# Queries and keys of the last tokens of tiles 8 to 15: computed ahead of the first segment and in segments 1 to 3, instead of in tiles 7 to 14

## The chip, the cores and the metric

The kernel runs on one NeuronCore of a Trainium2 chip. The metric is the device time of one launch, in microseconds. The kernel before takes 1615.39 us, the median of three runs (1613.97 to 1617.68).

## What is computed

Two layers, each made of a part A and a part B, on x of 2048 tokens x 512 features in bf16. Part A is attention with a recurrent memory: the sequence is cut into 64 segments of 32 tokens, and segment s attends over 8 memory rows and its own 32 tokens; the first 8 output rows are the memory of segment s + 1. So the 64 segments are a chain, and only the memory rows are carried along it.

```python
for s in range(n_seg):    # 64, one after the other
    h = jnp.concatenate([mem, xs], axis=1)    # 8 + 32 rows x 512
    q, k, v = (einsum('btd,dhe->bhte', h, W) for W in (Wq, Wk, Wv))   # 32 heads x 128
    scores = where(mask, einsum('bhqe,bhke->bhqk', q, k) * scale, -1e9)
    o = einsum('bhte,hed->btd', einsum('bhqk,bhke->bhqe', softmax(scores), v), Wo)
    mem = o[:, :8, :]; outs.append(o[:, 8:, :])
```

Part B is a gated MLP over the whole sequence (w_in, a 2048 x 2048 mix over the tokens, w_out). Each part is applied to the layer norm of x, and its result is added to x.

## The kernel before

**Tiles, segments, groups.** `a_block` (once per layer) walks the 64 segments. Four segments are a tile of 128 tokens (`tb`, 0 to 15; `j4` is the segment in its tile), four tiles are a group G. The matmuls of a segment itself (`psQ`, `psm`, `psK`, `psV` at L723) use 32 rows: 8 memory rows and the first 24 tokens. The last 8 tokens of a segment do not depend on the memory that is being made, so they are not done there: their queries, keys and values are made a tile at a time, 4 x 8 = 32 rows `hB`, one tile ahead, and put into `QTB`, `KTB` and `VB`/`VX` of that tile. That work comes in six pieces j = 0 to 5 (two halves of Q, of K and of V), 16 matmuls each of 32 weight columns by 512, four of them side by side in the array (`b_mms`, tile `psb`).

**The fill.** The pieces are the fill of the segment loop: `segment` calls `fill()` at three places (ahead of `pv(0)`; behind `spare1`; behind `last_out(0)`), and each call takes one step of a generator `more`. The order of the work on PE, DVE and ACT is the order in which the program states it (`manual_schedule` with ORDERED); SP's and POOL's order is the scheduler's.
- Segment 0 of layer one takes the values (`values`), segments 1 to 3 have `iter(())`: no fill.
- Tiles 1 to 3 (`tb < 4`) use `b_even`: in each segment half a piece in two steps (4 + 4 matmuls) and then a whole piece (16): 24 matmuls per segment. The last piece, j = 1, is turned by a DVE transpose (`turns`, L769), not by a DMA.
- Tiles 4 to 14 use `b_units` in the segments j4 = 0 to 2 (4, 8 and 20 matmuls) and `y_part` in j4 = 3, also 4 + 8 + 20: the product with Wo of the last tokens of the group before (`wo_last`, tile `pwB`), whose sum is added by DVE (`adds`, L857 and L863).
- Both layers use the same two patterns.

**Spare work.** `spare1`, `spare2` and `spare3` hold DVE and ACT work that isn't the segment's: layer norm of rows two tiles ahead (`x_stats`, `rows.apply`), and from tile 8 on the finished rows of eight tiles before (`ys`: in one segment two halves of an addition, `y_half` L238, in the next the statistics `y_stats` L147 and then `y_norm` L249).

**The start of layer one.** All weights come over GpSimd's DMA queue: Wq and Wk in halves r = 0, 1, then Wv (`a_open_qkv_weights`), then Wo in seven transfers (`_Wo.open`); a transfer is issued when the one eight places before it on that queue has landed. Meanwhile PE makes the pieces j = 0, 2 of tiles 0 and 1 and j = 1, 3 of tile 0, each as its half of the weights lands (`b_units(0, 6)`, `units`, and `b_units(1, 2, alone=True)`, `units1`), then segment 0, with the rest of tile 1's pieces in it (`ahead_of_wo`).

**The start of layer two.** At the end of part B, `wo.open(nc.sync)` queues 1.9 MB of Wo on SP's queue and then `ahead.spread` the four transfers that put the values of tile 0 into `VX`.

Of the kernel before, what the change touches and what calls it, by code (L numbers as in the profile page):

```python
# [14 lines left out]
P = 128  # L15
DM = 512
KT = 4
# [25 lines left out]
def _ln_consts(ctx, tc, c):  # L43
    nc = tc.nc
    cp = ctx.enter_context(tc.tile_pool(name="consts_ln", bufs=1))
    eps_t = cp.tile([P, 1], F32, name="eps_t")
    nc.vector.memset(eps_t[:], LN_EPS)
    c["eps_t"] = eps_t
    c["ident_bf"] = _identity(nc, cp)

    c["MV"] = [cp.tile([P, 16, 2], F32, name=f"MV{i}") for i in range(2)]
    c["RS"] = [cp.tile([P, 16], F32, name=f"RS{i}") for i in range(2)]


# [8 lines left out]

def _consts(ctx, tc, c, b_sp):
    nc = tc.nc
# [12 lines left out]
    nc.vector.tensor_reduce(out=is_own[:], in_=fourth[:], op=ALU.max, axis=mybir.AxisListType.X)  # L78
    nc.vector.tensor_copy(own, is_own[:].to_broadcast([P, 4, 16]))
    for q in range(0, P, 32):  # L80
# [104 lines left out]
class _Rows:  # L185


    def __init__(self, nc, pool, xd, xb_d, o_d, x_in):
        self.nc, self.pool, self.xd, self.xb_d, self.o_d, self.x_in = nc, pool, xd, xb_d, o_d, x_in
        self.xs, self.hT, self.y = {}, {}, {}  # L190

# [61 lines left out]
def b_block(tc, c, rows, front, xd, MV_out, RS_out, w_sp, w_out, S, first, ahead, wo, out_final=None):  # L253
# [4 lines left out]
    with ExitStack() as ctx:  # L258
# [231 lines left out]
def kernel(  # L490
# [31 lines left out]
    rows = _Rows(nc, rp, xd, xb_d, o_d, x_in)  # L522
    rows.vb_d = dram.tile([P, 8 * DH], BF16, name="vb_d")
    with tc.manual_schedule(engines=ORDERED):
        _act_table(nc)
        for tt in range(2):
            x = rp.tile([P, DM], F32, name="x0", tag=("ln_x", "y_x")[tt])[:, 0:DM // 2].bitcast(BF16)
            nc.sync.dma_start(x, x_in[tt * P:(tt + 1) * P, :])
            rows.xs[tt] = x
        m0 = rp.tile([2 * M, DM], BF16, name="m0", tag="y_o")  # L530
        nc.vector.memset(m0[:], 0.0)
        nc.sync.dma_start(m0[0:M, :], A_mem0.rearrange("b m d -> (b m) d"))
        rows.m0T = rp.tile([P, KT, 2 * M], BF16, name="m0T")
        wqkv, rest = a_open_qkv_weights(tc, ctx, A_Wq, A_Wk, A_Wv)
        c = {}
        _ln_consts(ctx, tc, c)
        MV, RS = c["MV"], c["RS"]
        with tc.tile_pool(name="turn_ps", bufs=3, space=PSUM) as turn_ps:

            def turn(out, x, n):  # L540
                ps = turn_ps.tile([P, KT * n], BF16, name=f"turn{n}", tag="turn")
                for kt in range(KT):
                    nc.tensor.transpose(ps[:, n * kt:n * kt + n], x[:, P * kt:P * kt + P], c["ident_bf"][0:n, 0:n])
                nc.scalar.copy(out, ps[:].rearrange("p (kt t) -> p kt t", kt=KT))
# [6 lines left out]
        _consts(ctx, tc, c, B_b_sp)  # L551
        rest()
# [16 lines left out]

def a_open_qkv_weights(tc, stack, Wq, Wk, Wv):  # L570
    nc = tc.nc
    wp = stack.enter_context(tc.tile_pool(name="a_wqkv", bufs=1, side="right"))
    w = [wp.tile([P, KT, HD], BF16, name=n) for n in ("Wq_sb", "Wk_sb", "Wv_sb")]

    def load(parts):
        for k, r in parts:
            srcv = (Wq, Wk, Wv)[k].rearrange("(kt p) h e -> p kt (h e)", p=P)
            for kt in range(KT):
                nc.gpsimd.dma_start(w[k][:, kt, 2048 * r:2048 * r + 2048], srcv[:, kt, 2048 * r:2048 * r + 2048])

    load(((0, 0), (1, 0)))
    return w, lambda: load(((0, 1), (1, 1), (2, 0), (2, 1)))

# [10 lines left out]
class _Wo:  # L594
# [4 lines left out]

    def open(self, eng, first=False):  # L600

# [5 lines left out]
        for k in reversed(range(len(WO_LOW))):  # L607
            n = WO_LOW[k]
            t = ctx.enter_context(self.tc.tile_pool(name=f"a_wo{k}", bufs=1, side="right")).tile([P, n, DM], BF16, name=f"Wo{k}")
            for h in range(n):  # L610
                self.parts[ends[k] - n + h] = t[:, h, :]
            self.parts[f"t{k}"] = t
        for k in range(len(WO_LOW)):
            eng.dma_start(self.parts[f"t{k}"][:], self.wov[:, ends[k] - WO_LOW[k]:ends[k], :])
# [63 lines left out]
def a_block(tc, c, rows, front, MV_in, RS_in, MV_out, RS_out, ahead, wo, S, first):  # L678
# [6 lines left out]
    with ExitStack() as ctx:  # L685
# [4 lines left out]
        for i in range(2):  # L690
            at, v = 0, list(front.old()) if i == 0 else []
            for k, n in enumerate(OLD_SIZES if i == 1 else ()):
                v.append(VBr[0] if k == 1 else old.tile([P, n], BF16, name=f"old{at}")[:])
                at += n
            oBr[i] = v[0].rearrange("p (h t) -> p h t", h=H)
            VBr[i] = v[1] if i else v[1].rearrange("p (i r e) -> p i r e", i=4, r=2)
# [39 lines left out]
        KXr = [[pers.tile([P, 4, 32], BF16, name=f"KX{i}{r}") for r in range(2)] for i in range(NKQ)]  # L736
        uT = [pers.tile([P, H, 32], BF16, name=f"uT{i}") for i in range(2)]
        for t in uT:
            (nc.vector if first else nc.gpsimd).memset(t[:], 0.0)
# [59 lines left out]
        def b_even(tb):  # L799

            bs = blk_state[tb]
            for j, others in ((4, (5, 0)), (3, (2, 1))):
                psA = accA.tile([P, 512], F32, name="psb")[:]
                for kt, other in zip((0, 2), others):
# [9 lines left out]
                    yield  # L814

        def wo_pairs(px, lhs):

# [25 lines left out]

        def y_part(G, q, last=False):

# [5 lines left out]
            pwB = accA.tile([P, DM], F32, name="pwB")  # L851
            for k, _ in enumerate(wo_last(parts, pwB)):
                if k in (0, 2):
                    yield

# [20 lines left out]

            adds.append(out)
            yield
# [25 lines left out]
        def prep_segment(s, eng=nc.gpsimd):  # L904
# [11 lines left out]
            seg_state[s] = dict(QQ=QQ, KX=KX, VX=bs["VX"])  # L916

        def fold(px, cross, t1, beside):
# [18 lines left out]
        def segment(s, fill, spare1, spare2, spare3, tail, loads):  # L937
# [177 lines left out]
            wo_pairs(px, uT_cur)  # L1115
            pw = psO[1][:, 0, 384:512]
            if begin:
                wo_rest(pw, uT_cur, hi=wo.low + 8)
                ahead_of_wo()
                wo_rest(pw, uT_cur, lo=wo.low + 8)  # L1120
            else:
                wo_rest(pw, uT_cur)
            cross = wk.tile([P, P], F32, name="cross", bufs=1)
            beside = nc.scalar.copy(cross[0:64, :], px[64:128, 128:256])
            Rt = segp.tile([P, 2, 512], F32, name="Rt", tag="Rt", bufs=1)
# [26 lines left out]
        if first:  # L1152
            for tb in range(2):
                ln_turn(tb, nc.scalar.copy)
            units, units1 = b_units(0, 6), b_units(1, 2, alone=True)
            for gen, n in ((units, 4), (units1, 2), (units, 4)):
                for _ in range(n):
# [27 lines left out]
        for s in range(NSEG):  # L1185
            tb, j4 = s // 4, s % 4
            if first and s == 0:
                more = values(units)
            elif j4 > 0 and tb == NB - 1:
                more = y_part(tb // 4, j4 - 1, last=True)  # L1190
            elif j4 == (3 if tb < NB - 1 else 0) and tb > 3:
# [33 lines left out]
            def spare2():  # L1225
                if first and s == 8:
                    c["cast_bsp"] = c["load_bsp"]()
                if first and s == 12:
                    c["cast_bsp"]()
                for y, added in ys:  # L1230
                    if added:
# [3 lines left out]

            def spare3():
                for y, added in ys:
                    if added:
# [10 lines left out]
            def tail():  # L1249
                if j4 == (3 if first and tb == 0 else 2 if tb < 4 else 1) and tb + 1 < NB:  # L1250
                    ahead.spread(blk_state[tb + 1]["VX"])
# [11 lines left out]

            def loads():
                if due and s < NSEG - 1 and (not ys or tb == NB - 1):
                    y = due.pop(0)
# [69 lines left out]
```

## Time and profile before

| what | value |
|---|---|
| three runs, median (lowest to highest) | 1615.39 us (1613.97 to 1617.68) |
| the profiled execution: its time, its span | 1618.87 us, 1617.1 us |
| between the span and that time | 1.8 us |
| granted TensorE clock, mean | 0.999 |
| busy: PE, PEld, DVE, ACT, POOL | 98%, 61%, 66%, 65%, 19% |
| layer one, segment 0 begins / segment 63 begins | 28.53 us / 672.57 us |
| layer two, segment 0 begins / segment 63 begins | 828.47 us / 1465.15 us |

A segment begins where its first `psQ` matmul does. Times inside the profile are microseconds from the span's start. Matmuls that run side by side are each counted with their own length, so the mean of one is longer than its share of the busy time. In the rows of engines, the first number is the start or the stretch, then the length, and `xN` is the number of instructions.

### The profile page before, as it was taken

The page shows a single profiled execution, that of the slowest core. Times are in us where ns is not written, and L with a number is a line of the kernel's source. Part 1 is how long each engine was busy: PE and PEld are TensorE (multiplying, and loading weights), DVE is VectorE, ACT ScalarE, POOL GpSimd, SP SyncE. Part 2 cuts the span into 40 slices and gives each one's busy share as a digit, 9 for nine tenths or more (in the row PEclk, how much of TensorE's full clock was granted, in tenths as well). Part 3 has the DMA queues.
Part 4 walks back from the last instruction along what each step waited for, and adds up shares of the span by engine and source line. Part 5 has one row for each costly group of instructions (what it writes and reads, how often), then busy time and mean ns, then how long its engine had stood idle before and what let it go on. Part 6 is the DMA issues. An engine that isn't in the chain of part 4 may idle for free.

```text
span 1617.1 us, 91209 instructions
## 1 busy us (share of the span) xinstructions
PE 1579.8 (98%) x41182; PEld 986.2 (61%) x41182; DVE 1066.0 (66%) x3050; ACT 1048.5 (65%) x2281; POOL 301.4 (19%) x667
## 2 busy tenths in 40 slices
PE   5899999999999999999999999999999999999999
PEld 2566666666666666666656666666666666665565
DVE  4577766667776776784456666666677667767722
ACT  3677777777777777660047777777777777776400
POOL 6111111112211221320021111111122122224000
PEclk9999999999999999999999999999999999999999
DMA  9312212213311332377951112212233223425696
GB/s 363 96 43 41 41 43 43 44 43 85 82 47 43 90 89 70 94 182 158 209 174 43 47 43 52 46 48 47 70 93 71 47 75 89 97 52 173 146 197 159
DMA packets 260525, 148.63 MB, mean 92 GB/s; under 512 B 193832, under 2 KB 236432, under 8 KB 260136
## 3 DMA queue, kind: packets, MB, share of 16 engines
q1 hardware_dynamic: 246904, 98.99, 27.5%
q0 software_dynamic: 13232, 43.82, 8.3%
q8 instruction: 322, 5.28, 1.4%
q14 instruction: 67, 0.55, 0.1%
HBM read 59.94 MB, written 37.45 MB: 60 GB/s over the span
## 4 chain that ended last, share of the span: by engine, by line
PE 92%; DMA 4%; issue 1%; DVE 1%; POOL 1%; ACT 0%; SPq 0%; POOLq 0%; DVEq 0%
PE psQ L723 13%; PE psK L723 13%; PE psb L723 10%; PE pg L397 9%; PE psO L828 7%; PE px L821 7%; PE psm L723 6%; PE psV L723 6%; PE pz L296 4%; PE pwB L840 3%; PE psO L1029 3%; PE py L440 2%; PE psT L1021 2%; PE psS L980 2%; DMA Wk_sb<-in_A_Wk_dram 1%
## 5 line engine op out<-in xcount | busy, mean ns | idle before, releaser
L723 PEld LDWEIGHTS <-hT 128*32 128x32 bf16 x12288 | 345.7, 97 | 261.6 <-DVE hT L929 13.9
L723 PE MATMUL psV<-Wv_sb,hT 128*32 128x512 bf16 x2048 | 165.8, 379 | 0.0
L957 DVE STREAM_TRANSPOSE QQ<-rows 128x256 f32<-128x256 f32 x256 | 113.1, 442 | 76.3 <-ACT rows L954 73.8
L954 ACT CAST rows<-psQ 128x512 bf16<-128x512 f32 x256 | 144.2, 591 | 28.9 <-PE psQ L723 26.2
L1050 DVE TENSOR_TENSOR uT<-psO,Rm 128x128 bf16<-128x128 f32 x256 | 74.7, 292 | 126.0 <-ACT Rm L1047 124.1
L989 ACT ACTIVATE S<-psS 128x224 bf16<-128x224 f32 x256 | 92.2, 360 | 96.3 <-PE psS L984 96.1
L397 PE MATMUL pg<-z,wspT 128*128 128x344 bf16 x1024 | 154.3, 309 | 0.0
L957 DVE STREAM_TRANSPOSE KA<-rows 128x256 f32<-128x256 f32 x256 | 113.5, 443 | 61.5 <-ACT rows L954 58.3
L1053 DVE TENSOR_TENSOR uT<-psO,Rt 128x384 bf16<-128x384 f32 x256 | 140.2, 548 | 17.9 <-ACT Rt L1129 15.8
L723 PE MATMUL psK<-Wv_sb,hT 128*32 128x512 bf16 x2048 | 152.0, 378 | 0.0
L1129 ACT ACTIVATE Rt<-Rt 128x512 f32<-128x512 f32 x256 | 147.3, 622 | 4.1
L828 PE MATMUL psO<-Wo_high,uT 128*32 128x128 bf16 x8192 | 141.6, 219 | 3.2 <-issue 3.0
L723 PE MATMUL psQ<-Wq_sb,hT 128*32 128x512 bf16 x2048 | 136.1, 381 | 4.4 <-DVE hT L929 2.8
L723 PE MATMUL psQ<-Wk_sb,hT 128*32 128x512 bf16 x2048 | 135.9, 381 | 0.0
L723 PE MATMUL psm<-Wq_sb,hT 128*32 128x512 bf16 x2048 | 135.1, 379 | 0.0
L723 PE MATMUL psK<-Wk_sb,hT 128*32 128x512 bf16 x2048 | 135.0, 379 | 0.0
L821 PE MATMUL px<-Wo,uT 128*32 128x256 bf16 x3840 | 133.2, 273 | 0.4
L1126 ACT ACTIVATE Rt<-psT 128x1024 f32<-128x1024 f32 x128 | 131.0, 1024 | 3.1
L828 PEld LDWEIGHTS <-uT 128*32 128x32 bf16 x8192 | 125.9, 97 | 11.3 <-issue 6.1
L397 PEld LDWEIGHTS <-wspT 128*128 128x128 bf16 x1024 | 100.0, 98 | 53.5 <-issue 0.4
L821 PEld LDWEIGHTS <-uT 128*32 128x32 bf16 x4096 | 107.6, 97 | 27.5 <-issue 1.3
L914 POOL COPY KX<-old 128x128 bf16<-128x128 bf16 x128 | 66.1, 544 | 274.4 <-PE psS L984 183.6
(202 smaller groups left out, 2875.6 us busy)
## 6 DMA issues: line engine op xcount, KB each, us to landing
o_d<-o_sb SPq DMA_DIRECT2D x126, 64.0 KB
vb_d<-front SPq DMA_DIRECT2D x31, 256.0 KB
VX<-vb_d SPq DMA_DIRECT2D x124, 64.0 KB
ln_x<-xd SPq DMA_DIRECT2D x26, 256.0 KB
y_o<-o_d POOLq DMA_DIRECT2D x22, 256.0 KB, 3.4
xd<-y_o POOLq DMA_DIRECT2D x22, 256.0 KB, 3.0
Wq_sb<-in_A_Wq_dram POOLq DMA_DIRECT2D x8, 512.0 KB, 8.6
Wk_sb<-in_A_Wk_dram POOLq DMA_DIRECT2D x8, 512.0 KB, 10.0
```

What stands on the lines that cost most here:

```text
L397: nc.tensor.matmul(pg[t][:, k, 0:344], lhsT=wsp[t][:, st, :], rhs=z(st, 344 * k, 344 * k + 344), start=(st == 0), stop=(st == NT - 1))
L723: return [nc.tensor.matmul(ps[32 * cg:32 * cg + 32, :], lhsT=lhs(kt, cg), rhs=rhs(kt, cg), start=(kt == 0), stop=(kt == KT - 1), tile_posi ...
L821: nc.tensor.matmul(px[at:at + 32, 0:256], lhsT=lhs[:, h, :], rhs=wo_rhs(h, slice(k + 2, None, -2) if h % 2 else slice(k, None, 2)), start= ...
L828: nc.tensor.matmul(pw[32 * cg:32 * cg + 32, :], lhsT=lhs[:, h, :], rhs=wo_rhs(h, cg), start=False, stop=(h == H - 1), tile_position=(0, 32 ...
L914: eng.tensor_copy(KX[r][:].rearrange("p g (k i) -> p i g k", i=4), bs["KTB"][:, r].rearrange("p (i g) k -> p i g k", i=4)[:, :, :, 8 * j4: ...
L954: return r, mms, copy(r[:].rearrange("p (n el two) -> p n el two", n=8, two=2), ps.rearrange("p (n two el) -> p n el two", n=8, two=2))
L957: nc.vector.transpose(out=(QQ[:, j % 2, :, 0:32] if j < 2 else KA[:, j % 2]).bitcast(F32).rearrange("p n q one -> p n (q one)"), in_=r[:]. ...
L989: return nc.scalar.activation(out=S[:, r], in_=psS[:, r, 0:224], func=ACT.Exp, scale=scale)
L1050: nc.vector.tensor_tensor(out=hview(uT_cur[:], r, 24, 32), in0=oview(r, 0, 8), in1=Rm[:, r].rearrange("p g (n q) -> p g n q", q=8), op=ALU ...
L1053: nc.vector.tensor_tensor(out=hview(uT_nxt[:], r, 0, 24), in0=oview(r, 8, 32), in1=rview(r, 0, 24), op=ALU.mult)
L1126: nc.scalar.activation(out=Rt[:], in_=psT[:], func=ACT.Ln)
L1129: nc.scalar.activation(out=rt, in_=rt, func=ACT.Exp, scale=-1.0)
```

## The change

Only layer one's part A changes in its work, and only for tiles 8 to 15 (groups 2 and 3), pieces j = 0 and j = 2 (first half of Q, first half of K).
- **Gather.** Two DMAs on GpSimd's queue, behind the second of Wq's transfers, bring the last 8 rows of each of a group's 16 segments: 128 rows x 512 for group 2 and for group 3. The transfers of Wk's first half are issued after the identity matrix is made instead of before.
- **Norm and turn.** DVE and ACT normalise both (`early_norm`, inside `_consts`), PE turns them and ACT copies them into the tile VX1, which is free until tile 1's values come.
- **Six pieces ahead of segment 0**, now with 128 rows at once (128 weight columns, 8 matmuls in each): j = 0 of both groups, j = 2 of group 2. ACT copies them, GpSimd's queue stores them to DRAM (`pre_d`, 512 KB per group and piece).
- **Four singles in segments 1 to 3**: j = 2 of group 3, 4 column chunks of 4 matmuls; in segments 1 and 2 one matmul in each of the first two fills and four in the third, in segment 3 four in the third.
- **Tiles 7 to 14 (`light`)**: `b_light` makes only the pieces 4, 5, 1, 3, one in the third fill of each segment, and spreads the 8 steps of `y_part` over the first two fills: 4 + 4 + 16 matmuls in each segment. The pieces 0 and 2 come by two DMA transposes out of `pre_d`, issued from SP. The piece j = 3 is turned by DVE, behind the addition `adds` of j4 = 3. The spread of VX moves from j4 = 1 to j4 = 2.
- **Spare work**: in the light tiles' segments j4 = 0 and 2, `spare2`'s second statistics go to `spare3`.
- Beside that: tile 1's values can be spread into VX1 only after the last single in segment 3; in segment 0 ACT's `cross` copy goes ahead of the last two pieces of tile 1; at the start of layer two the spread is issued ahead of Wo.

```diff
+EARLY = (2, 3)
+EARLY_CHUNKS = (0, 2)
...
-        wqkv, rest = a_open_qkv_weights(tc, ctx, A_Wq, A_Wk, A_Wv)
+        def gather():
+            for G in EARLY:
+                src = x_in[4 * P * G:4 * P * (G + 1), :].rearrange("(j r) c -> j r c", j=16)
+                nc.gpsimd.dma_start(x_last[G], src[:, SEG - M:SEG])
+        wqkv, second, rest = a_open_qkv_weights(tc, ctx, A_Wq, A_Wk, A_Wv, gather)
         _ln_consts(ctx, tc, c)
+        second()
...
+        def early_turn():
+            for k, G in enumerate(EARLY):
+                pT = (att, attO[1])[k].tile([P, 2 * DM * 2], BF16, name="pT")
+                for kt in range(KT):
+                    nc.tensor.transpose(pT[:, P * kt:P * kt + P], rows.early[G][:, P * kt:P * kt + P], c["ident_bf"][:])
+                nc.scalar.copy(early_lhs(G, slice(0, KT)).rearrange("p kt (k t) -> p kt k t", t=4),
+                               pT[:, 0:KT * P].rearrange("p (kt t k) -> p kt k t", kt=KT, t=4))
+        def early_mms(G, j, cg, ps, kts=range(KT)):
+            for kt in kts:
+                nc.tensor.matmul(ps, lhsT=early_lhs(G, kt), rhs=cols_rhs(w, j, kt, cg), start=(kt == 0), stop=(kt == KT - 1))
+        def early_units():
+            for n, (j, G, k) in enumerate((j, G, k) for j, G in ((0, 2), (0, 3), (2, 2)) for k in range(2)):
+                ps = (attO[0], attO[1], att)[n % 3].tile([P, 2, 512], F32, name="psP")
+                for i in range(2):
+                    early_mms(G, j, 2 * k + i, ps[:, i, :])
...
+        def b_light(tb, G, q):
+            bs = blk_state[tb]
+            for j in EARLY_CHUNKS:
+                t = bs[("QTB", "KTB")[j // 2]][:, j % 2]
+                nc.sync.dma_start_transpose(out=t.rearrange("p (i g) k -> p i (g k)", g=4),
+                                            in_=rows.pre_d[tb // 4, j][:, tb % 4, :].rearrange("t (i e) -> t i e", i=4))
+            steps = y_steps(G, q)
+            for n, j in enumerate((4, 5, 1, 3)):
+                for _ in range(2):
+                    next(steps)
+                    yield
+                psB = accB.tile([P, 512], F32, name="psb")[:]
+                b_mms(bs, j, psB, range(KT), j == 3)
+                copies.insert(0, lambda n=n, j=j, psB=psB: b_out(bs, n % 2, j, psB, j == 3, j == 5))
+                if n == 3:
+                    next(steps, None)
+                yield
...
-            for gen, n in ((units, 4), (units1, 2), (units, 4)):
+            for gen, n in ((units, 3), (None, 0), (units1, 1), (early, 4), (units, 1), (units1, 1), (early, 2), (units, 4)):
+                if gen is None:
+                    early_turn()
...
+            light = first and tb + 1 < NB and (tb + 1) // 4 in EARLY
...
             elif first and s == 1:
-                more = iter(())
+                more = early_rest()
+            elif light:
+                if j4 == 0:
+                    more = b_light(tb + 1, tb // 4 - 1, tb % 4)
...
-            wo.open(nc.sync)
-            ahead.spread(wo.VX[0])
+            wo.open(nc.sync, between=ahead.spread)
```

More of the change, by code (lines that the diff above doesn't have):

```diff
@@ L550, with early_norm @@
             turn(rows.m0T[:], m0[:], 2 * M)
-        _consts(ctx, tc, c, B_b_sp)
+        def early_norm():
+            MVe, RSe = c["MVe"], c["RSe"]
+            for k, G in enumerate(EARLY):
+                _stats(nc, rp, x_last[G], MVe[:, k, :])
+            _rstd_act(nc, RSe[:], MVe[:, :, 1], c)
+            for k, G in enumerate(EARLY):
+                xn = rp.tile([P, DM], BF16, name="ln_xn", bufs=2)
+                nc.vector.tensor_scalar(out=xn[:], in0=x_last[G], scalar1=MVe[:, k, 0:1], scalar2=RSe[:, k:k + 1],
+                                        op0=ALU.subtract, op1=ALU.mult)
+                rows.early[G] = xn
+        _consts(ctx, tc, c, B_b_sp, early_norm)
         rest()
@@ L612, in open @@
             self.parts[f"t{k}"] = t
+        if between is not None:
+            between(self.VX[0])
         for k in range(len(WO_LOW)):
@@ new lines, in early_rest, with out @@
+        def early_rest():
+            G, j = EARLY[1], EARLY_CHUNKS[1]
+            def out(cg, ps):
+                nc.scalar.copy(oflat[:, 512 * cg:512 * cg + 512], ps)
+            psA = accA.tile([P, 512], F32, name="psb")[:]
+            for kt, cg in zip((0, 2, KT), (1, 2, 3)):
+                for k in range(2):
+                    if kt < KT:
+                        early_mms(G, j, 0, psA, (kt + k,))
+                        if kt + k == KT - 1:
+                            copies.append(lambda: out(0, psA))
+                    yield
+                psB = accB.tile([P, 512], F32, name="psb")[:]
+                early_mms(G, j, cg, psB)
+                copies.insert(0, lambda cg=cg, psB=psB: out(cg, psB))
+                if kt == KT:
+                    early_stores.append((G, j, oflat[:, 0:2048], slice(0, 4)))
+                yield
@@ L875, in out, with y_part @@
                     store_last(G, 0, P, nc.sync)
-            adds.append(out)
+            for k, _ in enumerate(wo_last(parts, pwB)):
+                if k == 7:
+                    adds.append(out)
+                yield
+        def y_part(G, q, last=False):
+            for k, _ in enumerate(y_steps(G, q, last)):
+                if k in (0, 2):
+                    yield
             yield
@@ L1229, in spare2, with second_rows @@
                     c["cast_bsp"]()
+                if not (light and j4 % 2 == 0):
+                    second_rows()
+            def second_rows():
                 for y, added in ys:
@@ L1236, in spare3 @@
             def spare3():
+                if light and j4 % 2 == 0:
+                    second_rows()
                 for y, added in ys:
@@ L1264, in loads @@
             def loads():
+                if first and s in (0, 3):
+                    while early_stores:
+                        early_store(*early_stores.pop(0))
                 if due and s < NSEG - 1 and (not ys or tb == NB - 1):
```

61 lines of the change are left out of this document (43 added, 18 removed).

## The prediction

> **What bounds the kernel now.** I read the page's first parts, the stretches of single segments, and the start's timeline.
>
> ```profile
> span 1617.1 us, 91209 instructions
> PE 1579.8 (98%) x41182; PEld 986.2 (61%) x41182; DVE 1066.0 (66%) x3050; ACT 1048.5 (65%) x2281; POOL 301.4 (19%) x667
> PE 92%; DMA 4%; issue 1%; DVE 1%; POOL 1%; ACT 0%; SPq 0%; POOLq 0%; DVEq 0%
> ```
>
> PE is busy all the time and carries 92% of the chain of waits, but that does not say whether fewer matmuls in a segment make it shorter. Segments with different fill do. The stretches run from one segment's first `psQ` to the next's; xN on PE counts the matmuls, some of a neighbour's included.
>
> ```profile
> core 0: us, PE busy (x) PEld busy (x) DVE busy (x) ACT busy (x) POOL busy (x), PEclk, DMA share, GB/s
> 51.80:61.42 9.62, 8.73 (x276) 5.25 (x276) 6.53 (x21) 7.04 (x16) 1.56 (x3) 1.00 0.13 37
> 139.32:148.99 9.67, 9.67 (x304) 6.14 (x304) 6.87 (x23) 7.59 (x19) 0.00 (x0) 1.00 0.22 52
> 358.88:368.91 10.03, 10.03 (x313) 6.21 (x308) 6.91 (x22) 6.93 (x16) 1.74 (x4) 1.00 0.18 47
> 80.69:197.40 116.71, 116.52 (x3601) 72.61 (x3604) 81.61 (x246) 91.11 (x204) 16.15 (x39) 1.00 0.19 40
> 868.23:986.04 117.81, 117.28 (x3605) 72.93 (x3601) 80.34 (x236) 90.82 (x199) 17.59 (x45) 1.00 0.18 44
> 318.40:642.39 323.99, 323.05 (x9860) 207.71 (x9856) 234.35 (x695) 244.99 (x559) 66.40 (x150) 1.00 0.27 68
> ```
>
> Without fill (segment 1) 9.62 us, and PE idles 0.89 of it: the segment's own chain is the bound. With 24 matmuls of fill (`b_even`) 9.67: they lie in that gap. With 32 (`b_units`, `y_part`) 10.03: the last 8 stick out. So 24 are nearly free and the next 8 cost 0.36 us. The last three rows give means: 12 segments of `b_even` in either layer, 116.71/12 = 9.726 and 117.81/12 = 9.818, and the 32 segments of tiles 7 to 14, 323.99/32 = 10.125.
>
> The start, up to segment 1, is another regime:
>
> ```profile
> Wq_sb<-in_A_Wq_dram POOLq DMA_DIRECT2D x8, 512.0 KB, 8.6
> 19.21 0.53 POOL L579 DMA_DIRECT2D Wv_sb<-in_A_Wv_dram  x1 [0.75 <-DMA Wq_sb<-in_A_Wq_dram]
> 10.12 1.90 PE L723 MATMUL psb<-Wq_sb,hB 128*32 128x512 bf16 x16 [0.58 <-ACT m0T L544]
> 23.64 1.09 PE L723 MATMUL psb<-Wk_sb,hB 128*32 128x512 bf16 x8
> 25.36 0.40 PE L723 MATMUL psb<-Wk_sb,hB 128*32 128x512 bf16 x4 [0.63 <-DMA Wk_sb<-in_A_Wk_dram]
> 28.53 1.89 PE L723 MATMUL psQ<-Wq_sb,hT 128*32 128x512 bf16 x16 [1.49 <-DVE hT L215]
> 31.90 1.09 PE L723 MATMUL psm<-Wq_sb,hT 128*32 128x512 bf16 x16
> 32.81 1.04 PE L723 MATMUL psK<-Wk_sb,hT 128*32 128x512 bf16 x16
> 36.19 1.21 DVE L636 STREAM_TRANSPOSE VX<-ln_xn 128x128 bf16<-128x128 bf16 x4
> 38.89 0.71 DVE L633 STREAM_TRANSPOSE ln_xn<-front 128x512 bf16<-128x512 bf16 x1 [0.24 <-ACT front L759]
> 40.79 0.34 DVE L992 TENSOR_TENSOR E<-S,maskN 128x448 bf16<-128x448 bf16 x1
> 44.42 1.05 PE L821 MATMUL px<-Wo,uT 128*32 128x256 bf16 x30
> 46.45 0.29 PE L821 MATMUL px<-Wo_high,uT 128*32 128x256 bf16 x2 [0.98 <-DMA Wo_high<-in_A_Wo_dram]
> 50.84 0.23 PE L828 MATMUL psO<-Wo_high,uT 128*32 128x128 bf16 x1 [0.43 <-issue]
> 51.80 0.40 PE L723 MATMUL psQ<-Wq_sb,hT 128*32 128x512 bf16 x4 [0.74 <-DVE hT L929]
> ```
>
> Weights arrive at one 512 KB transfer per 1.28 us (issues of 0.53, each 0.75 after the last, released by a landing), and PE waits for them: at 25.36, at 46.45. Two pieces of 16 matmuls take 3.37 us from 28.53 to 31.90, 1.69 each, and the next 0.91 (to 32.81): half clock, then full.
>
> **The change, part by part.**
>
> *Light tiles, 32 segments.* A piece and its four quarters cost PE the same either way: a 32-row piece 0.91 us, times 4 tiles; 16 matmuls with 128 rows by the nearest row:
>
> ```profile
> L296 PE MATMUL pz<-front 128*128 128x512 bf16 x144 | 34.0, 379 | 0.0
> ```
>
> 34.0/144 = 0.236 each, 3.8 us. So no PE work is saved; it is moved from where it sticks out to where PE idles. Left in a light segment are 4 + 4 + 16 matmuls in the same three fills as in `b_even`. By the means: 32 x (10.125 - (9.726 + 9.818)/2) = 32 x 0.353 = **11.3 us** less (9.8 with layer two's mean alone, 12.8 with layer one's). The cover of the 24 is the gap of 0.89 us; without it they would cost up to 24 x 0.91/16 = 1.4 us a segment.
>
> What `b_even` doesn't have is the spare work and, at the tile's end, an addition and a turn on DVE in one segment:
>
> ```profile
> 158.66 1.05 PE L723 MATMUL psQ<-Wq_sb,hT 128*32 128x512 bf16 x16
> 160.41 0.70 DVE L769 STREAM_TRANSPOSE old<-rowsB 128x512 bf16<-128x512 bf16 x1
> 161.36 0.40 DVE L957 STREAM_TRANSPOSE KA<-rows 128x256 f32<-128x256 f32 x1
> 162.33 0.28 PE L980 MATMUL psS<-QQ,KA 128*32 128x40 bf16 x16
> 439.47 0.40 DVE L238 TENSOR_TENSOR y_o<-y_o,y_x 128x256 f32<-128x256 f32 x1
> 441.12 0.68 DVE L857 TENSOR_TENSOR yB<-pwB,yB 128x512 f32<-128x512 f32 x1
> ```
>
> The turn of `b_even` ends before KA does, 161.76, and PE asks for KA at 162.33: 0.57 to spare. The addition's 0.68 behind it overruns that by about 0.1 at each of 8 tile ends; where `y_half` (0.40) also lies ahead (segments j4 = 3 of tiles 8, 9, 12, 13) by about 0.3 more, and in the eight segments with `y_half` in `spare2` the copy of `cross` comes up to 0.2 late. 0.8 + 1.2 + 0.4 = **2.4 us** back (0 to 5: none if DVE's slack takes it, all 8 additions and 8 halves in full at most). The statistics moved to `spare3` leave `cross` alone and, with 0.57 to spare, cost nothing. The two DMA transposes from DRAM have 30 us; SP issues three transposes a tile instead of four.
>
> *The start.* GpSimd's queue gets 2 x 128 KB, so every weight behind is 256/512 x 1.28 = 0.64 us later: the lower bound. PE gets 48 matmuls with 128 rows and 8 turns. They can begin when the gathered tiles are normalised, by
>
> ```profile
> 2.96 0.69 DVE L140 BATCH_NORM_STATS2 bnst<-x 128x6 f32<-128x512 bf16 x1 [0.68 <-DMA x<-in_A_x_dram]
> 3.69 0.18 DVE L141 BATCH_NORM_AGGREGATE MV<-bnst 128x2 f32<-128x6 f32 x1
> 4.47 0.42 DVE L204 TENSOR_SCALAR ln_xn<-x,MV,RS 128x512 bf16<-128x512 bf16 x1 [0.60 <-ACT RS L118]
> L766 ACT CAST rowsB<-psb 128x512 bf16<-128x512 f32 x124 | 68.3, 572 | 15.6 <-PE psb L723 15.4
> ```
>
> Two statistics, 2 x 0.87, are hidden while PE makes the first piece; ACT takes the root only after copying that piece: its end 12.02 + 0.64 for the late weights + 0.57 + root 0.60 + scaling 0.42 = about 14.3. With the turns done, from 15.3, PE has 5 pieces and 48 singles, 5 x 0.91 + 48 x 0.22 = 15 us at full clock (0.22 is a quarter of a piece; 0.236 above). Half clock for about 4.3 us (an estimate, a little over the 3.4 from 28.53, where dense work begins, to 31.90, the first piece at full clock), then full, ends it at 32.4; with the 1.49 of row 28.53, segment 0 begins at 33.9, 5.4 late. Its first four pieces run at full clock, so the first piece of Wv ends near 33.9 + 5 x 0.89 = 38.3. Behind it DVE regroups the values: a copy of 0.57, then 0.71 + 1.21 to 40.8, other work of 1.3 (37.40 to 38.89, less the 0.24 of idling), the second half 1.9: E starts at 44.0 to 44.2, not 40.79, 3.4 late. So px starts at 47.8; having waited 0.98 for Wo, it ends 2.4 late, and the last matmul, which waited 0.43, and with it segment 1, come **2.0 us** late (0.64 to 4). The five stores follow Wo on GpSimd's queue and hold up no copy that is needed before segment 2. The moved `cross` copy gains nothing: PE's last Wo matmul ends as late.
>
> The Trainium skill ("TensorE: Matmul & The Clock Gate", Part 1) says that the array runs at half rate until a free-running window of about 3.4 us was busy; the 3.4 us from 28.53 to 31.90 agree. Its Part 4 says that transposes do not count as busy; no row here shows it. By that rule the eight turns could let one window pass: an estimate of 1.7 us more at the start, 3.7 in all, and a sum of -5.9.
>
> *Segments 1 to 3*: their singles fill the gap, 3 x (9.67 - 9.62) = **0.15** more. Tile 1's values wait for the last single, at 80.6, ahead of one o_d store on SP; four issues and a landing end near 86, and PE asks 6.2 into the segment (row 835.14 below), at 86.9: nothing, up to 1 us once.
>
> *Layer two's start.*
>
> ```profile
> 828.47 1.05 PE L723 MATMUL psQ<-Wq_sb,hT 128*32 128x512 bf16 x16
> 835.14 0.21 PE L1032 MATMUL psO<-E,VX 64*128 64x128 bf16 x1 [0.45 <-DMA VX<-vb_d]
> 835.58 0.21 PE L1032 MATMUL psO<-E,VX 64*128 64x128 bf16 x1 [0.23 <-DMA VX<-vb_d]
> 839.17 1.05 PE L723 MATMUL psQ<-Wq_sb,hT 128*32 128x512 bf16 x16
> ```
>
> This segment takes 10.70, 1.03 over 9.67, and waits for VX, which stands behind Wo on SP's queue. Ahead of it, it is in time, and Wo has until px: **0.9** less (0 to 1.0).
>
> *Sum*: -11.3 + 2.4 + 2.0 + 0.15 - 0.9 = **-7.6 us**: 1618.87 becomes 1611.3 for the profiled execution (1617.1 of span and 1.8 around it), which lay 3.5 over the median; from the median, 1615.39 - 7.6 = **1607.8**.
>
> **Rivals.**
> 1. *Slower: the half clock holds.* If PE's early block never turns to full clock, its 15 us take 30: segment 0 begins at 15.3 + 30 + 1.49 = 46.8, 12.9 later than in the forecast, -7.6 + 12.9 = +5.3, **1620.7**. From 7.6 later the gain is gone. For it: the rows from 10.12 and from 28.53 to 31.90 are at half clock. Against: rows 23.64 and 25.36, where dense pieces turned it. Chance 0.07.
> 2. *The change doesn't do it: light segments stay at 10.03*, because ACT or DVE work and not the 8 matmuls makes the difference. +2.0 + 0.15 - 0.9 = +1.25: **1616.6**. Against: segment 358.88 has less ACT work than 139.32 (6.93 to 7.59) and as much on DVE. 0.10.
> 3. *The start is hidden* behind the weights: only 0.64 late, -9.0: **1606.4**. 0.12.
> 4. *DVE's stalls at their upper bound* (5 for 2.4): -5.0, and the start's 4 for 2.0: -3.0: **1612.4**. 0.06.
>
> **How the numbers follow.** The forecast has 0.65, with its own bounds 1602.5 (12.8, no stalls, start 0.64: -12.9) to 1612. The range 1603 to 1613 takes in rivals 3 and 4 and leaves out 1 and 2. A measurement of this kernel can tell 0.2%, 3.2 us, from no change: faster is below 1612.2. Faster: 0.65 + 0.12 = 0.77; same: 0.10 + 0.06 = 0.16; slower: 0.07.
>
> **What would show it.** Light segments at 9.67 to 9.8 instead of 10.03, those behind a tile's end a little longer; segment 1 beginning between 52.4 and 55.8, with the early matmuls at 0.22 us from about 20 on; layer two's first segment near 9.8. Wrong would be: light segments at 10.03 (then the fill wasn't what stuck out), a start later than 56, or a DVE wait ahead of `psS` at every tile's end of 0.5 and more.

## The result and the profile after

| | before | after |
|---|---|---|
| time, median (lowest to highest), us | 1616.54 (1613.97 to 1618.95, 4 runs) | 1608.86 (1607.22 to 1610.67, 4 runs) |
| ratio | 1 | 0.9953, 95% interval 0.9933 to 0.9973 |
| profiled execution: time, span, us | 1618.87, 1617.1 | 1610.67, 1609.0 |

The change makes the kernel 7.7 us faster (4.4 to 10.8 by the interval); forecast were 7.6. The page of the changed kernel: span, busy time of the engines, shares of the chain that ended last.

```profile
span 1609.0 us, 90845 instructions
...
PE 1577.9 (98%) x40998; PEld 979.7 (61%) x40998; DVE 1068.8 (66%) x3064; ACT 1052.1 (65%) x2279; POOL 307.5 (19%) x674
...
PE 56%; DMA 1%; DVE 1%; issue 0%; ACT 0%; SPq 0%; POOL 0%; DVEq 0%; POOLq 0%
```

The page says little: PE was 98% busy before and is after, and the chain could be followed back only to 677 us, so its 56% can't be set against the 92% of before. The stretches of segments say more. In order: segment 1 and segment 3 (one by one and grouped early matmuls as fill), a light segment in the middle of tile 7, the last segment of tile 7, then tiles 1 to 3 of layer one, tiles 1 to 3 of layer two, and tiles 7 to 14. The columns are those of the same view of before.

```profile
53.19:63.19 10.00, 10.00 (x283) 6.11 (x283) 6.68 (x21) 7.28 (x16) 1.85 (x4) 1.00 0.43 69
73.19:83.02 9.83, 9.62 (x281) 5.59 (x280) 6.77 (x21) 7.33 (x17) 1.77 (x5) 1.00 0.11 26
331.64:341.31 9.67, 9.67 (x304) 5.85 (x304) 6.85 (x22) 7.31 (x17) 1.56 (x3) 1.00 0.15 37
351.53:361.56 10.03, 9.83 (x305) 6.14 (x305) 6.97 (x22) 7.60 (x18) 1.81 (x5) 1.00 0.27 38
83.02:200.84 117.82, 117.06 (x3602) 73.43 (x3601) 81.55 (x245) 91.79 (x206) 16.95 (x41) 1.00 0.20 47
863.82:980.38 116.56, 116.39 (x3604) 72.68 (x3604) 79.91 (x236) 90.69 (x199) 18.01 (x45) 1.00 0.18 45
321.98:636.07 314.09, 312.59 (x9605) 193.47 (x9601) 234.02 (x702) 238.81 (x543) 66.98 (x149) 1.00 0.27 67
```

The light segment takes 9.67, as forecast, and the 32 of them 314.09 instead of 323.99: 9.9 us less. Segment 1 takes 10.00 instead of 9.62 (forecast 9.67). The start of the changed kernel, by PE's timeline, with three of DVE's rows:

```profile
14.63 1.03 PE L872 MATMUL pT<-ident_bf,ln_xn 128*128 128x128 bf16 x8 [1.63 <-DVE ln_xn L572]
17.42 7.53 PE L881 MATMUL psP<-Wq_sb,VX 128*128 128x512 bf16 x32
26.73 3.63 PE L881 MATMUL psP<-Wk_sb,VX 128*128 128x512 bf16 x16
33.69 1.05 PE L753 MATMUL psQ<-Wq_sb,hT 128*32 128x512 bf16 x16 [1.49 <-DVE hT L219]
42.03 0.69 DVE L662 STREAM_TRANSPOSE ln_xn<-front 128x512 bf16<-128x512 bf16 x1
42.76 1.21 DVE L665 STREAM_TRANSPOSE VX<-ln_xn 128x128 bf16<-128x128 bf16 x4
43.89 0.35 DVE L1110 TENSOR_TENSOR E<-S,maskN 128x448 bf16<-128x448 bf16 x1
44.30 0.45 PE L1139 MATMUL psT<-E,ones 64*128 64x512 bf16 x4 [1.76 <-DVE E L1110]
47.53 1.05 PE L930 MATMUL px<-Wo,uT 128*32 128x256 bf16 x30
53.19 1.05 PE L753 MATMUL psQ<-Wq_sb,hT 128*32 128x512 bf16 x16 [1.11 <-ACT Rt L1245]
```

Segment 0 begins 5.16 later than before (33.69 to 28.53) but segment 1 only 1.39 later (53.19 to 51.80). Segment 0 now makes its pieces at full clock and waits for no weights. The longest wait left in it is the 1.76 for E, which stands behind the regrouping of the values on DVE. Layer two's first segment begins at 822.01 and ends at 834.31; its two idle times of PE are these:

```profile
828.99 0.26 PE L1098 MATMUL psS<-QQ,KA 128*32 128x40 bf16 x11 [1.86 <-issue]
832.81 0.84 PE L937 MATMUL psO<-Wo_high,uT 128*32 128x128 bf16 x45 [0.37 <-issue]
```

The waits for VX (0.45 and 0.23 before, the only idle time of PE in that segment) are gone, and the segment is longer nevertheless: 12.30 instead of 10.70. "issue" means that PE waited for nothing that the profile shows.

### The profile page after: what moved, and what is told of

It is laid out like the page before. It is cut to its first block, busy times and chain, and to the rows that moved or that the text cites. A ratio compares the mean times of both kernels' runs of the same rounds, so it can differ in the third digit from the quotient of the medians.

```text
span 1609.0 us, 90845 instructions
## 1 busy us (share of the span) xinstructions
PE 1577.9 (98%) x40998; PEld 979.7 (61%) x40998; DVE 1068.8 (66%) x3064; ACT 1052.1 (65%) x2279; POOL 307.5 (19%) x674
## 4 chain that ended last, share of the span: by engine, by line
PE 56%; DMA 1%; DVE 1%; issue 0%; ACT 0%; SPq 0%; POOL 0%; DVEq 0%; POOLq 0%
PE pg L401 9%; PE psQ L753 7%; PE psK L753 7%; PE psb L753 5%; PE pz L300 4%; PE psO L937 4%; PE px L930 3%; PE psV L753 3%; PE psm L753 3%; PE py L444 3%; PE pwB L949 2%; PE psO L1147 2%; PE psT L1139 1%; PE psS L1098 1%; PE pw L1422 0%; PE psS L1121 0%
## 5 line engine op out<-in xcount | busy, mean ns | idle before, releaser
L937 PEld LDWEIGHTS <-uT 128*32 128x32 bf16 x8192 | 123.0, 97 | 12.7 <-issue 3.6
L930 PEld LDWEIGHTS <-uT 128*32 128x32 bf16 x4096 | 104.0, 97 | 24.1 <-DVE uT L1168 1.2
```

What stands on the lines that cost most here:

```text
L930: nc.tensor.matmul(px[at:at + 32, 0:256], lhsT=lhs[:, h, :], rhs=wo_rhs(h, slice(k + 2, None, -2) if h % 2 else slice(k, None, 2)), start= ...
L937: nc.tensor.matmul(pw[32 * cg:32 * cg + 32, :], lhsT=lhs[:, h, :], rhs=wo_rhs(h, cg), start=False, stop=(h == H - 1), tile_position=(0, 32 ...
```

## Experiments

The experiments ran later, in three groups on two chips; in these groups the kernel before took 1621.4 to 1622.5 (medians of 11 to 21 runs, single ones from 1616.6 to 1628.7). Single segments are compared, since terms of 1 us don't show in whole times; their lengths are the distances of their first psQ in the timeline.

**The costs alone** (the light segments take the fill of before).

```
-            light = first and tb + 1 < NB and (tb + 1) // 4 in EARLY
+            light = False
```

> The early work, the singles and the new order at layer two's start stay, but tiles 7 to 14 fill their segments as the kernel before does (six pieces of their own each, y_part in the fourth segment), so that what was stored early is read by nobody. My theory: the light segments are where the whole gain comes from, and everything else costs: segment 1 at 53.2 (1.4 later than before), segments 1 to 3 at 10.0, 10.0, 9.84 (0.95 more), tiles 7 to 14 at 10.1 a segment (324 us in all), layer two's first segment at about 9.8 (0.9 less) unless its stall of 1.86 us comes again. Sum +1.4 to +2.4 against the kernel before. Rival: part of the gain comes from elsewhere (SP's queue, the moved copies), and this kernel is at or below the time of before.

Tiles 7 to 14 in this kernel:

```profile
322.05:647.53 325.48, 323.30 (x9860) 206.50 (x9856) 233.44 (x695) 245.12 (x559) 66.58 (x150) 1.00 0.29 68
```

That is the 323.99 of before again, but for scatter. Segment 1 begins at 53.73, segments 1 to 3 take 10.00, 10.00 and 9.84. So segment 1 comes 1.9 later than before and segments 1 to 3 take 1.0 more, while the tiles behind take no less: by segments the early work costs, and only the light segments pay for it. The time, 1.0012 of before (0.9997 to 1.0028; 0.5 us less to 4.5 more), doesn't tell this from no change. The rival, that part of the gain comes from elsewhere, isn't excluded by the interval, but no stretch of segments shows such a gain.

**Is it the number of matmuls?** (In light segments 4, 8 or 12 more matmuls ahead of the third fill's piece, by tile; their result is overwritten. An earlier form, which made the piece's own first pass again, gave no time.)

```
                 psB = accB.tile([P, 512], F32, name="psb")[:]
+                for _ in range((tb - 8) // 2):
+                    for cg in range(4):
+                        nc.tensor.matmul(psB[32 * cg:32 * cg + 32, :], lhsT=bs["hB"][:, 0, :], rhs=cols_rhs(w, j, 0, cg),
+                                         start=True, stop=True, tile_position=(0, 32 * cg))
                 b_mms(bs, j, psB, range(KT), j == 3)
```

> In light segments, matmuls of 32 rows are added ahead of the third fill's piece (their result is overwritten): none in tiles 7 and 8, 4 in tiles 9 and 10, 8 in tiles 11 and 12, 12 in tiles 13 and 14. My theory, by which 24 matmuls lie in PE's gap and more stick out: the shortest segments of these pairs of tiles come to 9.67, about 9.85, 10.05 and 10.3. Rival: it is not the number of matmuls but ACT's and DVE's work that made the segments of before 10.03, and all pairs stay at 9.67 to 9.7.

One of the shortest segments for each number added (none, 4, 8, 12), from tiles 7, 9, 11 and 13 (x on PE counts the matmuls):

```profile
324.01:333.68 9.67, 9.67 (x304) 5.77 (x296) 6.74 (x21) 6.70 (x16) 1.56 (x3) 1.00 0.06 18
424.78:434.66 9.88, 9.88 (x308) 6.34 (x304) 7.10 (x23) 7.29 (x18) 0.48 (x1) 1.00 0.28 88
495.07:505.19 10.12, 10.12 (x314) 7.09 (x308) 6.85 (x21) 7.28 (x17) 1.56 (x3) 1.00 0.16 36
587.95:598.26 10.31, 10.31 (x316) 6.27 (x312) 6.62 (x21) 7.55 (x18) 0.48 (x1) 1.00 0.22 70
```

0.21 more for each 4, and 4 x 0.91/16 is 0.23: beyond 24 matmuls each one sticks out almost in full. ACT's busy time grows too down these lines (6.70 to 7.55), but by the segment's place and not by the dose: in the changed kernel the last line's segment has 7.50 on ACT and takes 9.67. The theory holds, and its reason too; the rival (9.67 throughout) falls.

**The singles in segments 1 to 3** (column group 0 whole, in segment 1's third fill).

```
-            for kt, cg in zip((0, 2, KT), (1, 2, 3)):
-                for k in range(2):
...
+            for cg in (1, 2, 3):
+                yield
+                yield
+                if cg == 1:
+                    psA = accA.tile([P, 512], F32, name="psb")[:]
+                    early_mms(G, j, 0, psA)
...
```

> The four matmuls of the first early column group, which stood one by one in the first two fills of segments 1 and 2, are put together into the third fill of segment 1, which then has 8 of them; segments 2 and 3 keep 4 in the third fill and nothing in the first two. My theory: a lone full-width matmul between tiled ones costs 0.1 to 0.17 by itself, so segments 2 and 3 come to 9.62 to 9.75 (10.00 and 9.84 in the changed kernel), and segment 1, with 4 more in the third fill, to about 9.9 to 10.6. Rival: what makes these segments longer is full-width work in the third fill or the copies behind it, and segment 2 stays at 10.0.

Segments 1 to 3:

```profile
53.62:64.32 10.70, 10.32 (x283) 6.26 (x283) 7.50 (x23) 8.03 (x17) 2.11 (x4) 1.00 0.39 73
64.32:74.16 9.84, 9.58 (x280) 5.58 (x280) 6.04 (x19) 7.46 (x18) 1.69 (x4) 1.00 0.04 10
74.16:84.00 9.84, 9.59 (x280) 5.62 (x280) 6.78 (x21) 7.31 (x17) 1.78 (x5) 1.00 0.11 24
```

Both theories were half right. Without its two lone matmuls segment 2 is 0.16 shorter (10.00 to 9.84), so these cost 0.08 each; but the group of four by itself costs 0.22 over the 9.62 without fill, where 24 narrow matmuls cost 0.05. Four more of them cost another 0.86, nearly their full 4 x 0.22 (the 16 at 26.73 in the changed kernel take 3.56 to the next row). All in all this kernel's three segments are 0.5 longer than those of the changed one. Full-width matmuls fill PE's gap badly, and their own length is most of the reason, not the copies behind them: the first row is the four in segment 3 of this kernel (one record is missing), which ends at 84.00, the second the 16 narrow ones of segment 13 of the kernel before, which ends at 178.01.

```profile
83.04 1.04 PE L881 MATMUL psb<-Wk_sb,VX 128*128 128x512 bf16 x3
177.15 1.05 PE L723 MATMUL psb<-Wq_sb,hB 128*32 128x512 bf16 x16
```

The four begin 8.88 into their segment and take 0.96 to its end, the 16 begin at 8.81 and take 0.86; neither row waits for another engine. Of the 0.17 between the two prices the length is 0.10, the later start the rest.

**The order at layer two's start** (VX behind Wo again).

```
-            wo.open(nc.sync, between=ahead.spread)
+            wo.open(nc.sync)
+            ahead.spread(wo.VX[0])
```

> At layer two's start the spread of VX stands behind Wo on SP's queue again, as in the kernel before. My theory: its first segment waits 0.45 and 0.23 for VX and takes 10.7 again; what made it 12.30 in the changed kernel is a stall of PE that has nothing to do with the order and needn't come. Rival: in the changed kernel the new order itself brought the stall of 1.86 (Wo later, or the transfers on top of one another), so that here the segment is at 10.7 and the new order is a loss of 1.6.

PE's idle times in its first segment, which takes 10.98:

```profile
832.33 0.26 PE L1099 MATMUL psS<-QQ,KA 128*32 128x40 bf16 x11 [0.54 <-issue]
836.15 0.84 PE L938 MATMUL psO<-Wo_high,uT 128*32 128x128 bf16 x45 [0.37 <-issue]
```

Neither theory: no wait for VX although it stands behind Wo, and an issue gap at the same matmul of psS, only shorter. So a gap there doesn't need the new order. With VX ahead this segment took 12.30, 11.38, 10.32, 10.69, 11.20, 12.74, 10.76, 11.19 and 12.04 in nine profiles (mean 11.4), with VX behind 10.70 and 10.98. The new order gained nothing that can be seen; whether it makes the gaps longer, two profiles against nine don't tell.

**The start, longer** (16 of the early matmuls made twice).

```
+                if n < 2:
+                    for i in range(2):
+                        early_mms(G, j, 2 * k + i, ps[:, i, :])
```

> The matmuls of the first two early units are made twice (16 full-width matmuls more ahead of segment 0, with the same result), which by 0.235 each is 3.8 us more on PE there. My theory: in the changed kernel what sets segment 1's beginning is no longer Wo's arrival but the chain from segment 0's start through DVE's E and ACT, so segment 0 begins at about 37.5 and segment 1 at about 56.5 to 57.5, nearly all of the 3.8 later. Rival: the start is still bound by the weights behind segment 0 (Wo's last part landed at 50.6), and segment 1 comes less than 2 us later than 53.2.

```profile
35.97 1.05 PE L753 MATMUL psQ<-Wq_sb,hT 128*32 128x512 bf16 x16 [1.56 <-DVE hT L219]
46.58 0.45 PE L1142 MATMUL psT<-E,ones 64*128 64x512 bf16 x4 [1.77 <-DVE E L1113]
51.03 1.09 PE L933 MATMUL px<-Wo,uT 128*32 128x256 bf16 x30
```

Segment 0 begins at 35.97, segment 1 at 56.72. A kernel whose early turns began about as soon (13.69 against 13.55) and that has the same segment 0 of 20.76, the one with the spare work undone, has 32.29 and 53.05. So 3.7 us more ahead of segment 0 are 3.7 more at segment 1: from a segment 0 that begins at 32.3 on, the weights bind nothing there any more, and the chain through E does. The next microsecond of early work would be paid in full.

**Work in segment 0's gap** (8 of the 16 early matmuls of segments 1 to 3 between pv(0) and psT, the other 8 in the third fills of segments 1 and 2; run twice).

```
             pv(0)
+            if begin:
+                early_gap()
...
+        def early_gap():
+            G, j = EARLY[1], EARLY_CHUNKS[1]
+            t = wk.tile([P, DM], F32, name="yB", bufs=1)[:].bitcast(BF16)
+            for cg in range(2):
+                ps = (accA, accB)[cg].tile([P, 512], F32, name="psb")[:]
+                early_mms(G, j, cg, ps)
+                nc.scalar.copy(t[:, 512 * cg:512 * cg + 512], ps)
+            early_stores.append((G, j, t, slice(0, 2)))
```

> Two of the four early column groups that segments 1 to 3 carry (8 full-width matmuls, 1.9 us) are made in segment 0 instead, ahead of psT, where PE waited 1.76 us for E; their copies go to ACT at once; the other two stand in the third fills of segments 1 and 2, nothing in the first two fills. My theory: the gap takes them (segment 1 begins within 0.4 us of 53.2 to 54.1), segments 1 and 2 come to 9.84, as a group of 4 in the third fill cost 0.2, and segment 3 to 9.62: 0.5 us less in all, too little for the time of the whole kernel, which should stay at 0.994 to 0.998 of the kernel before. Rival: the two copies on ACT, or px's bank, bring segment 0 a delay of 0.5 to 1.1 that eats it.

Segments 1 to 3 in the first of the two runs:

```profile
52.56:62.40 9.84, 9.58 (x279) 5.88 (x280) 6.68 (x21) 7.30 (x16) 2.14 (x4) 1.00 0.50 97
62.40:72.24 9.84, 9.58 (x280) 5.61 (x281) 6.86 (x22) 7.59 (x19) 1.70 (x4) 1.00 0.03 10
72.24:81.89 9.65, 8.76 (x278) 5.30 (x277) 6.56 (x21) 7.13 (x17) 2.42 (x5) 1.00 0.29 78
```

As expected, 29.33 for 29.84, with segment 0 at 19.52: the 8 matmuls are free there. 0.9935 of the kernel before (0.9911 to 0.9959).

> The changed kernel as it is, once more, beside the next one on one chip. My theory: 0.993 to 0.997 of the kernel before; in segment 0 its time depends on where the 3.41 us windows of the clock's record fall against the gap of 1.76 us ahead of psT: 19.5 us (as in two profiles of this segment 0) or 20.76 with one window at half clock ahead of px (as in four); layer two's first segment shows issue gaps of 0.5 to 2 us that end about 1.4 us after an instruction packet has landed. Rival: the 1.26 comes from a wait for Wo's weights, so that with 20.76 the clock's record stays at full and px shows a wait for a DMA.

> The kernel with 8 of the full-width matmuls in segment 0's gap, as it is, once more. My theory: with the gap filled no window of the clock's record is idle enough, so segment 0 takes 19.5 whatever the windows' place, with no half clock between 40 and 52 us; segments 1 to 3 take 9.84, 9.84 and 9.65; that is 0.5 to 1.8 us less than the kernel beside it, within the scatter of whole times (0.992 to 0.997 of the kernel before). Rival: the 19.5 of its first profile was the windows' place alone, and the half clock comes here (20.76) as often as without the fill.

The changed kernel came to 0.9960 (0.9946 to 0.9975), the one with the filled gap beside it to 0.9947 (0.9931 to 0.9963). It is the fastest seen here, but the intervals overlap: that it is faster than the change as given is shown by its segments (29.33 and 29.48 for 29.84; the last of the three took 9.81 in the second run, not the 9.65 expected), not by its time.

Segment 0 without the fill took 19.50, 19.50 and 19.55 in three profiles, 20.75 to 20.77 in four and 21.93 in one. The clock's record tells which: it changes in steps of 3.41 us. Below are, each in order of time, the step with the wait for E and the one behind it in the kernel with the spare work undone (20.76), then the same two in the changed kernel (19.50), then the one with psT in the second run of the filled gap, then three steps in a row of the kernel with 21.93 (the one with more matmuls by tile, whose start is that of the changed kernel).

```profile
40.40:43.81 3.41, 1.63 (x60) 0.87 (x48) 2.62 (x8) 1.36 (x5) 1.63 (x4) 1.00 1.03 348
43.81:47.22 3.41, 2.73 (x32) 0.98 (x28) 0.29 (x1) 1.02 (x3) 1.84 (x4) 0.50 1.04 346
```

```profile
42.27:45.69 3.42, 1.66 (x44) 0.98 (x42) 2.14 (x7) 1.31 (x5) 2.62 (x5) 1.00 1.04 350
45.69:49.10 3.41, 2.72 (x92) 1.95 (x88) 0.65 (x3) 1.44 (x3) 0.01 (x1) 1.00 1.02 352
```

```profile
40.25:43.66 3.41, 3.27 (x63) 1.61 (x63) 2.82 (x8) 2.47 (x6) 1.95 (x4) 1.00 1.03 347
```

```profile
40.61:44.02 3.41, 1.73 (x66) 0.75 (x54) 3.38 (x11) 1.91 (x5) 1.77 (x4) 1.00 1.03 346
44.02:47.43 3.41, 2.48 (x34) 1.25 (x35) 1.37 (x6) 0.59 (x2) 1.87 (x4) 0.50 1.04 350
47.43:50.85 3.42, 2.73 (x36) 1.22 (x32) 0.00 (x0) 0.83 (x2) 0.00 (x0) 0.50 1.01 373
```

A step with 1.63 busy is followed by one at half clock (so in all four kernels with 20.76), one with 1.65 to 1.68 is not (in the three with 19.5). Where the steps fall against the gap goes with it: beginning 8.11 to 8.40 us into segment 0 (6.30 in the kernel with 21.93) they led to half clock, at 8.54, 8.58 and 9.46 they didn't. In the second run of the filled gap the step begins 8.05 into the segment, next to the bad ones; it has 3.27 busy, and no half clock follows. So the fill does away with it, and the rival (place alone) falls, by this one profile. The expectation held for the clock, then, but not for the 19.5: that run's segment 0 is 20.11, because it began early enough (32.20) to wait for Wo again.

```profile
47.44 0.29 PE L935 MATMUL px<-Wo_high,uT 128*32 128x256 bf16 x2 [0.20 <-DMA Wo_high<-in_A_Wo_dram]
```

This row begins 1.25 behind the start of px, and 0.78 in the changed kernel; that is 0.47 of the 0.61, and 0.15 came before psT. The rival of the other run falls: px waited for no DMA in any kernel with 20.76, and the clock's record is at half there. The Trainium skill ("TensorE: Matmul & The Clock Gate", Part 1) has the free-running window of about 3.4 us, and the trace agrees; it lets the clock fall after a window that is idle, and here one that was 48% busy did it (1.63 of 3.41). Busy time, as this profile has it, isn't quite what is counted: in the kernel with 21.93 a step with 1.73 was followed by half clock, and for two steps.

**The spare work undone** (`second_rows` always in `spare2`).

```
-                if not (light and j4 % 2 == 0):
-                    second_rows()
+                second_rows()
...
-                if light and j4 % 2 == 0:
-                    second_rows()
```

> The second half of the rows' work in light segments goes back from the third spare place to the second. My theory: it stands ahead of the fold of px on DVE again, so in segments 0 and 2 of a tile where it is due the fold comes 0.2 to 0.4 late, the third fill's piece waits for px's bank, and these segments lengthen to 9.9 to 10.1; tiles 7 to 14 come to 1 to 4 us more than in the changed kernel (314 to 318). Rival: DVE's slack takes it, and nothing in these segments moves.

The 16 segments concerned (j4 = 0 and 2 of tiles 7 to 14) take 160.35 together; in seven profiles with the spare work as changed they took 156.2 to 158.3, mean 157.4. All 32 take 317.46, inside the 314.1 to 318.7 of the seven. The 3 us stand in the segments named, but not in the wait that the theory has: PE's idle times over 0.05 in these 16 segments are 2.36 in all and every one is an issue gap, none a wait for px's bank; in the seven they are 0 to 1.05, issue gaps too. So the theory isn't shown, and the order of the spare work may be worth nothing.

## Why the prediction was right, point by point

- **Light segments**: right in size, and in the mechanism of the gain. Forecast -11.3 with 2.4 given back by DVE, -8.9; the first profile shows -9.9, the seven profiles a mean of 316.3 against 324.7 in the two with the old fill, -8.5. The -11.3 rests on 8 matmuls that stick out for some 0.36 a segment, and the doses show that (8 added ones cost 0.45). Given back are 316.3 - 32 x 9.772 = 3.6 (1.4 in the first profile), between the bounds 0 and 5, but not where the prediction put it: it had most of it at the tiles' ends, and in the first profile the segments j4 = 0 to 3 lie 1.2, 1.3, 0.9 and 1.3 over eight times 9.67. The last segments of tiles 7 and 14 do take 10.03 and 10.04, but PE idles there ahead of the third fill's piece, 0.20 and 0.24 for the fold of px on DVE, not ahead of psS:

```profile
360.70 1.05 PE L753 MATMUL psb<-Wk_sb,hB 128*32 128x512 bf16 x16 [0.20 <-DVE t L1040]
```

- **Start**: forecast +2.0, measured +1.39. The steps came as forecast: segment 0 at 33.69 (33.9), E at 43.89 (44.0 to 44.2), px at 47.53 (47.8). Full clock came at 18.4, not 19.6, while the first 32-row piece behind the turns began at 15.59, not 15.3. What the prediction did not have is the half clock in the middle of segment 0, in five of the eight profiles without the fill. The seven profiles with exactly this early work have segment 1 at 53.05 to 56.24 (mean 54.0), +1.3 to +4.4: the last, the kernel with 21.93, lies past the bound of 4 and past the 56 that the prediction named as a sign of being wrong. That the first profile had no such step is luck. The 1.7 us that the prediction set beside its sum, should the eight turns not count as busy, is answered below: they count.
- **Singles in segments 1 to 3**: the term that was mis-sized, +0.96 instead of +0.15. The step that failed took the 24 narrow matmuls' price (0.05) for 4 to 6 full-width ones.
- **Layer two's first segment**: forecast -0.9, and this step failed. The VX wait went, as forecast, but it was only 0.68, and it took nothing off the segment: PE's issue gaps, 0.45 to 2.66 together in the nine profiles, stand in the same segment, as they do with the old order in one profile of two (0.91). Whether the new order makes them longer stays open.
- **Rivals**: no half clock held over the early block (rival 1): from 18.38 the record is at full. Light segments did not stay at 10.03 (rival 2). The start was not hidden (rival 3). DVE's stalls and the start were not at their upper bounds in the first profile (rival 4; 1.4 and 1.39).
- **Sum**: by means the terms give -8.5 + 2.2 + 0.95 + 0.6 = -4.8 (the last is 11.4 against 10.84 in layer two's first segment); measured were -7.7 (4.4 to 10.8 less) and, beside the kernel before in the last group, -6.5 (4.1 to 8.8 less). The two misses, 0.8 and 1.5, are smaller than what the same code scatters by: the rest of layer two, whose code is as before, took 625.98 before, 621.87 after, and up to 628.3 in the others. The 8.1 between the two profiled spans are -9.9 in light segments, +1.4 at the start, +1.0 in segments 1 to 3, +1.2 in tiles 1 to 6, +1.6 in layer two's first segment, -4.1 in the rest of layer two and +0.7 elsewhere. That -7.6 met -7.7 so closely is luck; that the time fell by some microseconds is not, since the light segments alone gave 8.5 to 9.9.

## What to carry to other kernels

Where segments repeat, read the cost of a few matmuls from segments that differ only in their fill: what lies in PE's gap is free, what sticks out costs its full time, and moving work across that edge is worth more than its count. Price a matmul by its own shape: four full-width ones cost 0.22 in a segment that took 24 narrow ones, 16 of them in the same place, for 0.05. Before adding work to a start that waits for weights, ask which chain takes over when the weights stop binding; from there on each microsecond costs one, and an idle time of half a clock window on that chain can cost a further 1.26 (2.43 in one profile). And read a result on a term of 1 us from several profiles: the first one here showed neither the half clock nor the scatter of the issue gaps.

## What the runs showed of the hardware

- The clock falls back in mid-kernel after a 3.41 us window only half idle, as shown above; the 24 or 25 matmuls that start in the next window take about twice as long (the 16 of a piece 1.90 instead of 1.05).
- As far as these windows show, turning up takes a busier window than not falling back, and turns on PE count. The record's first entry is the turn to full clock; the windows ahead of it are counted back from there. In the kernel before, windows of matmuls alone with 2.58 and 2.27 us busy (14.94 to 18.35, 18.35 to 21.76) were followed by half clock, one with 2.75 (21.76 to 25.18) by full. In the second run of the filled gap the window from 12.95 to 16.36, 2.77 busy with the eight turns (1.03) and 1.80 without them, was followed by full. Were turns not counted, 1.80 would have sufficed there where 2.58 did not before.
- PE's "issue" gaps come from its instruction stream, as far as the traces show. The stretch ahead of the gap of 1.86 in the changed kernel, and ahead of the gap of 2.01 at the same matmul in the one with the spare work undone, in the view of DMA queues (packets, MB, share of 16 engines):

```profile
q1 hardware_dynamic: 322, 0.46, 102.9%
q8 instruction: 1, 0.02, 5.3%
```

```profile
q1 hardware_dynamic: 330, 0.49, 102.4%
q8 instruction: 1, 0.02, 4.8%
```

```profile
830.81 0.25 PE L1098 MATMUL psS<-QQ,KA 128*32 128x40 bf16 x11 [2.01 <-issue]
```

Each stretch (826.5 to 827.7, 828.3 to 829.6) holds the one instruction packet of 16 KB that landed, at 827.64 and 829.41, 1.35 and 1.40 ahead of the gap's end. In the eleven traces all 127 issue gaps over 0.25 us behind segment 0 end 1.2 to 1.6 us after such a packet has landed, and in layer one's segments these packets come 4.2 us apart on average, so chance would put about one gap in ten there. At layer two's start the DMA engines are full with Wo and xd (the first rows), which fits gaps being longest there; that a lighter load would shorten them wasn't tried.
